# Top-32 attention before a capacity-limited mixture of experts: weights from scores computed a second time, keys on partitions

## The chip, the cores and the metric

The kernel runs on one core of a Trainium2 chip. A core has engines that run side by side, each with its own queue of instructions worked off in order: TensorE (matrix products, written to PSUM), VectorE, ScalarE and GpSimd (element-wise work and reductions), and queues that start transfers between HBM and SBUF. They meet through semaphores. In profiles TensorE is PE (PEld is its weight load), VectorE DVE, ScalarE ACT, GpSimd POOL. The metric is the time of one execution on the device in microseconds; lower is better.

## The reference

Only the first block is touched by the change: attention in which each query keeps its 32 largest scores. Its output, with the heads side by side, feeds a mixture of experts (argmax gate, at most 80 tokens per expert, two products), which stays as it is.

```python
batch, n_heads, seq, head_dim = (8, 8, 576, 64)
...
def _attn_ref(q, k, v):
    top_k = 32
    scale = 1.0 / np.sqrt(D)
    scores = scale * np.matmul(q, k.transpose(0, 1, 3, 2))
    kth = np.partition(scores, -top_k, axis=-1)[..., -top_k:-top_k + 1]
    mask = scores >= kth
    scores = np.where(mask, scores, -1000000000.0)
    scores = scores - np.max(scores, axis=-1, keepdims=True)
    attn = np.exp(scores)
    attn = attn / (np.sum(attn, axis=-1, keepdims=True) + 1e-09)
    return np.matmul(attn, v).astype(np.float32)
```

All inputs and outputs are fp32. A row's 32nd largest score has to be found exactly: it decides which keys count.

## The kernel before

Heads are taken in pairs, 32 pairs in all. A pair's q and k are turned so that head dimension lies on partitions, 64 for each of the two heads. A *unit* is 128 queries of one head against all 576 keys: four per head, and a ninth unit that holds the last 64 queries of both heads. That makes 288 units. The steps of one unit:

```python
def front(self, n, t):          # scores of two heads, queries on partitions
    ps = [self.ps_s.tile([P, 2, 512], F32, name="sp", tag="sp") for _ in range(2)]
    for j in range(2):
        for h in range(2):
            nc.tensor.matmul(ps[h][..., j, :HS], lhsT=qT[d, t * P : t * P + m], rhs=kT[d, j * HS : (j + 1) * HS], ...)
    for h in range(2):          # one copy per head, scaled by 2**-48
        nc.scalar.activation(self.s[u]..., ps[h]..., Act.Copy, scale=TINY)

def parts(self, i):             # the 8 largest of each of 6 stretches of 96 keys
    for j in range(NG):
        nc.vector.max(out=cand[:, j, :], in_=s[:, j * S // NG : (j + 1) * S // NG])
        yield

def search(self, i):
    for r in range(G0 // 8):    # the 24 largest of the 48 candidates
        nc.vector.max(out=dst, in_=cand)
        yield
        if r < G0 // 8 - 1:
            nc.vector.match_replace(out=cand, in_to_replace=dst, in_values=cand, imm_value=LOW)
            yield
    # how many scores reach the 24th candidate, and s with those out of the way
    nc.vector.scalar_tensor_tensor(out=y, in0=s, scalar=w9[:, 7:8], in1=s, op0=Alu.is_ge, op1=Alu.subtract,
                                   accum_out=self.cnt[:, i : i + 1])
    yield
    nc.vector.max(out=w9[:, 8:], in_=self.y.pop(i))      # the next 8
    yield
    nc.vector.scalar_tensor_tensor(out=pick, in0=past, scalar=self.cnt[:, i : i + 1], in1=w9[:, 7:],
                                   accum_out=self.thr[i], op0=Alu.is_equal, op1=Alu.mult)   # the 32nd largest
    yield

def turn_sign(self, i):
    nc.gpsimd.tensor_scalar(y, y, -1.0, 0.0, op0=Alu.mult, op1=Alu.add)

def drop(self, i):              # d = s where it counts, far below the rest
    nc.scalar.activation(low, s, Act.Relu, bias=thr[:, 0:1], scale=-1.0)
    nc.gpsimd.tensor_scalar(low, low, BIG, top[:, 0, 0:1], op0=Alu.mult, op1=Alu.add)
    nc.gpsimd.tensor_tensor(out=self.d[i], in0=s, in1=low, op=Alu.subtract)

def turn_w(self, i):            # keys to partitions, five chunks of 116, then exp
    for c in range(NC):
        nc.tensor.transpose(w[:CK, c * P : (c + 1) * P], dd[:, k0 : k0 + CK], ident)
    nc.scalar.activation(self.wT[i]..., w[:CK, : NC * P], Act.Exp, scale=scale / TINY)

def back(self, i, n, t, h):     # product with v and a column of ones, 64 queries at a time
    for c, (j, hh, r, p) in order:
        nc.tensor.matmul(pw[...], lhsT=wT[:, c, r : r + TL], rhs=self.vb[...][:, c, hh, :], ...)
    nc.scalar.copy(xu[:, t, h, :], pw[:, o : o + D + 1])
```

The program is laid out step by step, one unit entering at each step, so that VectorE's instructions of neighbouring units lie between each other (`G` is a chunk maximum of the newest unit, the small letters are the next instructions of older ones):

```python
for c in "GbGcGdGeGgGfah":
    ...
self.drop(i - 3)
self.turn_sign(i - 1)
self.turn_w(i - 4)
if t == 1 and h == 0: self.turn(n + 1)
if units[i + 2][2] != 1: self.front(*units[i + 2][:2])
self.back(i - 4, *units[i - 4])
...                             # norm: division, output rows, gate logits of finished head pairs
```

In the text, *chunk maximum* is the instruction `G`, *whole-row maximum* the one over `y`, *front* the score products, *group* what `turn_w` puts on TensorE, *product with V* what `back` does.

Of the kernel before, what the change touches and what calls it, by code (L numbers as in the profile page):

```python
# [21 lines left out]
BIG = 2.0 ** 100  # L22
# [3 lines left out]
def kernel(  # L26
# [28 lines left out]
    CK = 116  # L55
    NC = 5
    DUP = NC * CK - S
# [32 lines left out]
    past = count_up("past", TOP_K - G0 + 1, pattern=[[-1, TOP_K - G0 + 1]], base=TOP_K, channel_multiplier=0)  # L90
# [23 lines left out]
    class Attention:  # L114


        def __init__(self, stack, lean):
            self.lean = lean
            pool = lambda name, bufs, **kw: stack.enter_context(tc.tile_pool(name=name, bufs=bufs, **kw))
            self.nat, self.qkp, self.rows = pool("nat", 1), pool("qkp", 2), pool("rows", 2)  # L120
            self.small, vpool = pool("small", 4), pool("vpool", 1)
            self.ps_s, self.ps_w = pool("ps_s", 2, space=PSUM), pool("ps_w", 2, space=PSUM)
            self.qk, self.turned, self.lg = {}, {}, {}
            self.s, self.top, self.y, self.thr, self.d, self.w, self.wT, self.xu = ({} for _ in range(8))
            if not lean:

                self.cnt = vpool.tile([P, NU], F32, name="cnt")

            self.vb = []
            for j in range(1 if lean else 3):  # L130
                t = vpool.tile([CK, NC, 2, D + 1], F32, name=f"vb{j}")
                nc.gpsimd.memset(t[:, :, :, D : D + 1], 1.0)
                nc.gpsimd.memset(t[:DUP, NC - 1, :, :], 0.0)
                self.vb.append(t)

            self.xTb = []
            for j in range(1 if lean else 2):
                t = vpool.tile([P, NK * P], F32, name=f"xT{j}")
                nc.gpsimd.memset(t[:, S:], 0.0)
                self.xTb.append(t)  # L140

        def load(self, n, b, hp):
# [11 lines left out]
            t = self.vb[n % len(self.vb)]  # L154
            e = (NC - 1) * CK
            for h in range(2):
                nc.sync.dma_start(
                    t[:, : NC - 1, h, :D], v[one, 2 * hp + h, :e, :].rearrange("o (c p) d -> p (o c) d", p=CK))
            nc.sync.dma_start(
                t[DUP:CK, NC - 1, :, :D], v[one, 2 * hp : 2 * hp + 2, e:, :].rearrange("o h p d -> p (o h) d"))  # L160
            self.qk[n] = tiles

        def turn(self, n):

            ts_ = []
            for src, name in zip(self.qk.pop(n), ("qT", "kT")):
                src = src.rearrange("p c h d -> p c (h d)")
                t = self.qkp.tile([P, S], F32, name=name, tag=name)
                ps = self.ps_w.tile([P, 1024], F32, name="tp", tag="w")
                for c in range(NF):  # L170
                    nc.tensor.transpose(ps[:, c * P : (c + 1) * P], src[:, c, :], ident)  # L171
                nc.tensor.transpose(ps[:, NF * P : S], src[:TL, NF, :], ident[:TL, :TL])
# [4 lines left out]
        def front(self, n, t):  # L177
# [4 lines left out]
            ps = [self.ps_s.tile([P, 2, 512], F32, name="sp", tag="sp") for _ in range(2)]  # L182
            off = [0, 0] if t < NF else [0, TL]
            for j in range(2):
                for h in range(2):
                    d = slice(D * h, D * h + D)
                    nc.tensor.matmul(ps[h][off[h] : off[h] + m, j, :HS], lhsT=qT[d, t * P : t * P + m],  # L187
                                     rhs=kT[d, j * HS : (j + 1) * HS], start=True, stop=True)
            for h in range(2):
                u = i + h if t < NF else i  # L190
                if t < NF or h == 0:
                    self.s[u] = self.rows.tile([P, S], F32, name="s", tag="s", bufs=3 if self.lean else 7)
                o = slice(off[h], off[h] + m)
                nc.scalar.activation(self.s[u][o, :].rearrange("p (j c) -> p j c", j=2), ps[h][o, :, :HS], Act.Copy,  # L194
                                     scale=TINY)
# [10 lines left out]
        def search(self, i):  # L206
# [4 lines left out]
            for r in range(G0 // 8):  # L211
                dst = top[:, r, :] if r < G0 // 8 - 1 else w9[:, :8]
                nc.vector.max(out=dst, in_=cand)  # L213
                yield
                if r < G0 // 8 - 1:
                    nc.vector.match_replace(out=cand, in_to_replace=dst, in_values=cand, imm_value=LOW)  # L216
                    yield
            y = self.y[i] = self.rows.tile([P, S], F32, name="y", tag="y")
            nc.vector.scalar_tensor_tensor(out=y, in0=s, scalar=w9[:, 7:8], in1=s, op0=Alu.is_ge, op1=Alu.subtract,  # L219
                                           accum_out=self.cnt[:, i : i + 1])  # L220
            yield
            nc.vector.max(out=w9[:, 8:], in_=self.y.pop(i))  # L222
            yield
            pick = self.small.tile([P, TOP_K - G0 + 1], F32, name="pick", tag="pick")
            self.thr[i] = self.small.tile([P, 1], F32, name="thr", tag="thr")
            nc.vector.scalar_tensor_tensor(out=pick, in0=past, scalar=self.cnt[:, i : i + 1], in1=w9[:, 7:], accum_out=self.thr[i],  # L226
                                           op0=Alu.is_equal, op1=Alu.mult)
            yield

        def turn_sign(self, i):  # L230
            y = self.y[i]
            nc.gpsimd.tensor_scalar(y, y, -1.0, 0.0, op0=Alu.mult, op1=Alu.add)  # L232

        def search_all(self, i):
# [9 lines left out]
            self.thr[i] = top[:, TOP_K // 8 - 1, 7:8]  # L244

        def drop(self, i):

            s, top, thr = self.s.pop(i), self.top.pop(i), self.thr.pop(i)
            low = self.rows.tile([P, S], F32, name="low", tag="low")
            nc.scalar.activation(low, s, Act.Relu, bias=thr[:, 0:1], scale=-1.0)  # L250
            nc.gpsimd.tensor_scalar(low, low, BIG, top[:, 0, 0:1], op0=Alu.mult, op1=Alu.add)  # L251
            self.d[i] = self.rows.tile([P, S], F32, name="d", tag="d")
            nc.gpsimd.tensor_tensor(out=self.d[i], in0=s, in1=low, op=Alu.subtract)  # L253

        def turn_w(self, i):

            dd = self.d.pop(i)
            w = self.w[i] = self.ps_w.tile([P, 1024], F32, name="pw", tag="w")
            for c in range(NC):
                k0 = c * CK if c < NC - 1 else S - CK  # L260
                nc.tensor.transpose(w[:CK, c * P : (c + 1) * P], dd[:, k0 : k0 + CK], ident)  # L261
            self.wT[i] = self.rows.tile([CK, NC, P], F32, name="wT", tag="wT")
            nc.scalar.activation(self.wT[i].rearrange("p c r -> p (c r)"), w[:CK, : NC * P], Act.Exp, scale=scale / TINY)  # L263

        def back(self, i, n, t, h):

            wT, pw = self.wT.pop(i), self.w.pop(i)
            if t == 0 and h == 0:
                self.xu[n] = self.rows.tile([P, NK, 2, D + 1], F32, name="xu", tag="xu")
            xu = self.xu[n]  # L270
            o = NC * P
            parts = [(0, h, 0, 0), (0, h, TL, TL)] if h < 2 else [(0, 0, 0, 0), (1, 1, TL, 0)]
            order = [(c, x) for c in range(NC) for x in parts] if h < 2 else [(c, x) for x in parts for c in range(NC)]
            for c, (j, hh, r, p) in order:
                nc.tensor.matmul(pw[p : p + TL, o + j * (D + 1) : o + (j + 1) * (D + 1)], lhsT=wT[:, c, r : r + TL],  # L275
                                 rhs=self.vb[n % len(self.vb)][:, c, hh, :], start=(c == 0), stop=(c == NC - 1))
            if h < 2:
                nc.scalar.copy(xu[:, t, h, :], pw[:, o : o + D + 1])  # L278
            else:
                nc.scalar.copy(xu[:TL, t, :, :].rearrange("p h d -> p (h d)"), pw[:TL, o : o + 2 * (D + 1)])  # L280

        def norm(self, n, b, hp, bi, nb):
# [20 lines left out]
            ps = self.ps_w.tile([P, 1024], F32, name="tp", tag="w")  # L303
            for c in range(NF):
                nc.tensor.transpose(ps[:, c * P : (c + 1) * P], xn[:, c, :], ident)
            nc.tensor.transpose(ps[:, NF * P : S], xn[:TL, NF, :], ident[:TL, :TL])
            xT = self.xTb[n % len(self.xTb)]
            nc.scalar.copy(xT[:, :S], ps[:, :S])
            yield
            ps = self.ps_w.tile([P, 1024], F32, name="tp", tag="w")  # L310
# [48 lines left out]
        def run(self, slow):  # L359
# [7 lines left out]
            later = []  # L367

            def step(i):
                if i < NU:  # L370
# [3 lines left out]
                    if t in (1, 3) and h == 0 and slow and n:  # L374
                        slow.pop(0)()
                    first[i] = self.parts(i)
                for c in "GbGcGdGeGgGfah":
# [8 lines left out]
                    elif i - (2 if c in "gh" else 1) in second:  # L386
                        next(second[i - (2 if c in "gh" else 1)])
                if 0 <= i - 3 < NU:
                    self.drop(i - 3)
                if 0 <= i - 1 < NU:  # L390
                    self.turn_sign(i - 1)
                if 0 <= i - 4 < NU:
                    self.turn_w(i - 4)
                if i < NU:
                    if t == 1 and h == 0 and n + 1 < NP:
                        self.turn(n + 1)
                    if i + 2 < NU and units[i + 2][2] != 1:
                        self.front(*units[i + 2][:2])
                if 0 <= i - 4 < NU:
                    self.back(i - 4, *units[i - 4])  # L400
# [294 lines left out]
```

## Time and profile before

The time is 1470.59 us, the median of three runs (1466.25 to 1477.74). The profiled execution spans 1469.7 us. Busy time of each engine in two stretches of it, with the mean granted TensorE clock:

| stretch, us | PE | DVE | ACT | POOL | PEclk |
|---|---|---|---|---|---|
| 600 to 800 (attention) | 149.42 | 186.82 | 111.76 | 149.64 | 0.79 |
| 1340 to 1470 (experts) | 97.99 | 26.14 | 10.39 | 15.39 | 0.84 |

How the lines of a profile are read: a group's line has source line, engine and operation, what is written from what, shapes, the number of instructions, then busy time in us and mean duration in ns, then the engine's idle time just before them and what ended most of it. In the timeline, the columns are start and length in us, engine, line, operation and count; instructions of one line that follow each other are merged. Durations of instructions in a pipeline overlap, so the distance from start to start may be shorter than the duration. The clock record says which share of its full clock TensorE was granted, in periods of 3.413 us; it takes only the values 0.5 and 1.0 here.

### The profile page before, as it was taken

The page shows a single profiled execution, that of the slowest core. Times are in us where ns is not written, and L with a number is a line of the kernel's source. Part 1 is how long each engine was busy: PE and PEld are TensorE (multiplying, and loading weights), DVE is VectorE, ACT ScalarE, POOL GpSimd, SP SyncE. Part 2 cuts the span into 40 slices and gives each one's busy share as a digit, 9 for nine tenths or more (in the row PEclk, how much of TensorE's full clock was granted, in tenths as well). Part 3 has the DMA queues.
Part 4 walks back from the last instruction along what each step waited for, and adds up shares of the span by engine and source line. Part 5 has one row for each costly group of instructions (what it writes and reads, how often), then busy time and mean ns, then how long its engine had stood idle before and what let it go on. Part 6 is the DMA issues. An engine that isn't in the chain of part 4 may idle for free.

```text
span 1469.7 us, 32849 instructions
## 1 busy us (share of the span) xinstructions
PE 1068.7 (73%) x11502; PEld 799.3 (54%) x11502; DVE 1241.3 (84%) x5385; ACT 721.5 (49%) x1341; POOL 961.4 (65%) x1072
## 2 busy tenths in 40 slices
PE   6677777777777777777777777787777777631887
PEld 4455555555555555555555555555555555531887
DVE  6999999999999998899999989989999889948110
ACT  4555555555555555555555555554555555410010
POOL 4777777777777777777777777777776787710110
PEclk8888877887788787787877778777887778755799
DMA  5023222222122112222222111101111110030470
GB/s 130 2 91 91 91 76 62 62 62 62 33 58 60 53 48 60 62 62 62 62 62 62 48 32 30 30 12 32 34 34 33 33 34 9 10 123 0 130 266 27
DMA packets 153294, 85.59 MB, mean 58 GB/s; under 512 B 117024, under 2 KB 135456, under 8 KB 153120
## 3 DMA queue, kind: packets, MB, share of 16 engines
q1 hardware_dynamic: 152096, 80.78, 19.5%
q0 software_dynamic: 1024, 2.62, 0.6%
q8 instruction: 93, 1.52, 0.4%
q14 instruction: 81, 0.66, 0.2%
HBM read 63.19 MB, written 20.19 MB: 57 GB/s over the span
## 4 chain that ended last, share of the span: by engine, by line
DVE 58%; POOL 15%; PE 14%; issue 10%; ACT 1%; DMA 0%; SPq 0%; POOLq 0%; DVEq 0%; ACTq 0%
DVE y L219 18%; DVE cand L202 12%; DVE w L222 9%; DVE pick L226 8%; POOL d L253 7%; DVE cand L216 4%; POOL low L251 4%; POOL y L232 4%; DVE top L213 3%; PE yp L603 3%; PE sp L187 2%; PE pw L275 2%; PE pw L261 2%; DVE w L213 1%; DVE top L478 1%
## 5 line engine op out<-in xcount | busy, mean ns | idle before, releaser
L253 POOL TENSOR_TENSOR d<-s,low 128x576 f32<-128x576 f32 x288 | 459.5, 1596 | 24.0
L202 DVE MAX8 cand<-s 128x8 f32<-128x96 f32 x1728 | 416.4, 241 | 12.9 <-ACT s L194 12.9
L261 PE MATMUL pw<-ident,d 128*116 128x128 f32 x1440 | 275.8, 335 | 167.9 <-POOL d L253 167.5
L275 PE MATMUL pw<-vb,wT 116*64 116x65 f32 x5760 | 294.6, 252 | 136.1 <-ACT wT L263 136.1
L275 PEld LDWEIGHTS pw<-vb,wT 116*64 116x64 f32 x5760 | 250.4, 161 | 262.7 <-ACT wT L263 202.7
L251 POOL TENSOR_SCALAR low<-low,top 128x576 f32<-128x576 f32 x288 | 223.5, 776 | 208.8 <-ACT low L250 184.7
L219 DVE SCALAR_TENSOR_TENSOR y<-s,w 128x576 f32<-128x576 f32 x288 | 347.7, 1207 | 0.0
L261 PEld LDWEIGHTS pw<-ident,d 128*116 128x116 f32 x1440 | 193.6, 165 | 201.5 <-POOL d L253 190.7
L250 ACT ACTIVATE low<-s,thr 128x576 f32<-128x576 f32 x288 | 223.9, 777 | 129.2 <-DVE pick L226 126.5
L222 DVE MAX8 w<-y 128x8 f32<-128x576 f32 x288 | 213.3, 741 | 86.4 <-POOL y L232 86.4
L187 PE MATMUL sp<-kT,qT 64*128 64x288 f32 (+1 forms) x1280 | 279.3, 563 | 1.5 <-ACT s L194 0.7
L232 POOL TENSOR_SCALAR y<-y 128x576 f32<-128x576 f32 x288 | 196.6, 683 | 98.8 <-DVE y L219 98.8
L194 ACT ACTIVATE s<-sp 128x576 f32<-128x576 f32 (+1 forms) x320 | 193.7, 648 | 129.2 <-PE sp L187 128.2
L263 ACT ACTIVATE wT<-pw 116x640 f32<-116x640 f32 x288 | 201.0, 698 | 56.0 <-PE pw L261 51.3
L226 DVE SCALAR_TENSOR_TENSOR pick<-past,cnt,w 128x9 f32<-128x9 f32 x288 | 183.6, 638 | 0.1
L187 PEld LDWEIGHTS sp<-kT,qT 64*128 64x128 f32 (+1 forms) x1280 | 145.4, 233 | 63.1 <-issue 41.7
L213 DVE MAX8 top<-cand 128x8 f32<-128x48 f32 x576 | 111.5, 194 | 0.1
L278 ACT COPY xu<-pw 128x65 f32<-128x65 f32 x256 | 55.7, 217 | 110.0 <-PE pw L275 107.0
L216 DVE MATCH_REPLACE8 cand<-top,cand 128x48 f32<-128x48 f32 x576 | 107.2, 186 | 0.0
L615 POOL DMA_INDIRECT out_dram<-y,idx_s x8 | 7.4, 930 | 79.0 <-DVE y L614 79.0
L213 DVE MAX8 w<-cand 128x8 f32<-128x48 f32 x288 | 53.8, 187 | 0.0
L171 PE MATMUL tp<-ident,kn 128*128 128x128 f32 x128 | 34.7, 425 | 23.1 <-ACT qT L173 22.6
(160 smaller groups left out, 799.1 us busy)
## 6 DMA issues: line engine op xcount, KB each, us to landing
w<-in_moe_w_dram SPq DMA_DIRECT2D x32, 512.0 KB
w<-in_moe_w_dram SPq DMA_DIRECT2D x8, 2048.0 KB
out_dram<-zero SPq DMA_DIRECT2D x9, 1024.0 KB
qn<-in_q_dram SPq DMA_DIRECT2D x64, 128.0 KB
kn<-in_k_dram SPq DMA_DIRECT2D x64, 128.0 KB
xd<-xn SPq DMA_DIRECT2D x32, 256.0 KB
vb<-in_v_dram SPq DMA_DIRECT2D x64, 116.0 KB
vb<-in_v_dram SPq DMA_DIRECT2D x32, 56.0 KB
```

What stands on the lines that cost most here:

```text
L187: nc.tensor.matmul(ps[h][off[h] : off[h] + m, j, :HS], lhsT=qT[d, t * P : t * P + m], rhs=kT[d, j * HS : (j + 1) * HS], start=True, stop=True)
L202: nc.vector.max(out=cand[:, j, :], in_=s[:, j * S // NG : (j + 1) * S // NG])
L213: nc.vector.max(out=dst, in_=cand)
L219: nc.vector.scalar_tensor_tensor(out=y, in0=s, scalar=w9[:, 7:8], in1=s, op0=Alu.is_ge, op1=Alu.subtract, accum_out=self.cnt[:, i : i + 1])
L222: nc.vector.max(out=w9[:, 8:], in_=self.y.pop(i))
L226: nc.vector.scalar_tensor_tensor(out=pick, in0=past, scalar=self.cnt[:, i : i + 1], in1=w9[:, 7:], accum_out=self.thr[i], op0=Alu.is_equal ...
L232: nc.gpsimd.tensor_scalar(y, y, -1.0, 0.0, op0=Alu.mult, op1=Alu.add)
L250: nc.scalar.activation(low, s, Act.Relu, bias=thr[:, 0:1], scale=-1.0)
L251: nc.gpsimd.tensor_scalar(low, low, BIG, top[:, 0, 0:1], op0=Alu.mult, op1=Alu.add)
L253: nc.gpsimd.tensor_tensor(out=self.d[i], in0=s, in1=low, op=Alu.subtract)
L261: nc.tensor.transpose(w[:CK, c * P : (c + 1) * P], dd[:, k0 : k0 + CK], ident)
L275: nc.tensor.matmul(pw[p : p + TL, o + j * (D + 1) : o + (j + 1) * (D + 1)], lhsT=wT[:, c, r : r + TL], rhs=self.vb[n % len(self.vb)][:, c, ...
```

## The change

Weights are needed with keys on partitions. Before, the masked scores were made with queries on partitions and turned by transposes. After, the scores are computed a second time with keys on partitions, and the mask (0 for a kept key up to the row's maximum, 1 for a dropped one, in bf16) is multiplied into the same PSUM by `minus`, the identity times -2**48, so that exp gives zero for what is dropped. The count of scores above the 24th candidate comes from ScalarE's Sign and its sum, and the same signs, multiplied by `s` on GpSimd, put the larger scores out of the way; GpSimd's other two passes and ScalarE's Relu go. Two heads share a score copy (`ps` is now one tile of four banks) and a group (`ab`, two banks, one buffer; `cc`, one bank, two buffers).

```diff
+    minus = const.tile([P, P], BF16, name="minus")
+    nc.scalar.mul(minus, ident, -1.0 / TINY)
...
-            self.ps_s, self.ps_w = pool("ps_s", 2, space=PSUM), pool("ps_w", 2, space=PSUM)
+            self.ps_s, self.ps_w, self.ps_c = (pool(n, k, space=PSUM) for n, k in (("ps_s", 1), ("ps_w", 1), ("ps_c", 2)))
...
+            nc.scalar.activation(s[:, : g * S].rearrange("p (j c) -> p j c", c=HS), ps[:, : 2 * g, :HS], Act.Copy, scale=TINY)
...
+                if r == G0 // 8 - 1:
+                    y = self.rows.tile([P, S], F32, name="y", tag="y", bufs=3)
+                    cnt = self.small.tile([P, 1], F32, name="cnt", tag="cnt")
+                    nc.scalar.activation(y, s, Act.Sign, bias=w9[:, 7:8], scale=-1.0, accum_out=cnt)
+                    nc.gpsimd.tensor_tensor(out=y, in0=s, in1=y, op=Alu.mult)
...
-            nc.vector.scalar_tensor_tensor(out=y, in0=s, scalar=w9[:, 7:8], in1=s, op0=Alu.is_ge, op1=Alu.subtract,
-                                           accum_out=self.cnt[:, i : i + 1])
...
-        def turn_sign(self, i):
-            y = self.y[i]
-            nc.gpsimd.tensor_scalar(y, y, -1.0, 0.0, op0=Alu.mult, op1=Alu.add)
...
-            nc.scalar.activation(low, s, Act.Relu, bias=thr[:, 0:1], scale=-1.0)
-            nc.gpsimd.tensor_scalar(low, low, BIG, top[:, 0, 0:1], op0=Alu.mult, op1=Alu.add)
-            nc.gpsimd.tensor_tensor(out=self.d[i], in0=s, in1=low, op=Alu.subtract)
+            self.mask[i] = self.rows.tile([P, S], BF16, name="mask", tag="mask", bufs=3)
+            nc.vector.tensor_scalar(self.mask[i], s, self.thr[:, i : i + 1], top[:, 0, 0:1], op0=Alu.is_lt, op1=Alu.add)
...
-                nc.tensor.transpose(w[:CK, c * P : (c + 1) * P], dd[:, k0 : k0 + CK], ident)
+            for c in range(NK):
+                for h in range(2):
+                    nc.tensor.matmul(ab[:, h, c, :m] if c < NF else cc[d, :m], lhsT=masks[h][:, ks], rhs=eye[h],
+                                     start=True, stop=False)
+                for h in range(2):
+                    nc.tensor.matmul(ab[:, h, c, :m] if c < NF else cc[d, :m], lhsT=kT[d, ks], rhs=qT[d, rows],
+                                     start=False, stop=True)
+            nc.scalar.activation(wT[:, : 2 * NF, :m], ab..., Act.Exp, scale=scale)
+            nc.scalar.activation(wT[:, 2 * NF, :m], cc[:, :m], Act.Exp, scale=scale)
...
-                for c in "GbGcGdGeGgGfah":
+                back = dict(a=0, b=1, c=1, d=1, e=1, g=2, h=3, m=3)      # how many steps a letter lies behind
+                for c in "GbGcGdGehGmGga":                                # h: pick, m: mask, g: whole-row maximum
...
+                j = i - 3
+                if 0 <= j < NU and units[j][2]:
+                    self.turn_w(*units[j][:2])
+                self.fronts = i + 2 < NU and units[i + 2][2] != 1
+                if self.fronts:
+                    self.front(*units[i + 2][:2])
+                elif due:
+                    self.turn(due.pop())
+                j = i - 4
+                if 0 <= j < NU and units[j][2]:
+                    self.back(*units[j][:2])
```

Products with V take 128 keys per chunk and a last chunk of 64 in place of five of 116.

## The prediction

> **What bounds the kernel now.** I read the page first: engines, granted clock, costliest groups.
>
> ```profile
> PE 1068.7 (73%) x11502; PEld 799.3 (54%) x11502; DVE 1241.3 (84%) x5385; ACT 721.5 (49%) x1341; POOL 961.4 (65%) x1072
> ...
> PEclk8888877887788787787877778777887778755799
> ...
> L253 POOL TENSOR_TENSOR d<-s,low 128x576 f32<-128x576 f32 x288 | 459.5, 1596 | 24.0
> ...
> L261 PE MATMUL pw<-ident,d 128*116 128x128 f32 x1440 | 275.8, 335 | 167.9 <-POOL d L253 167.5
> ...
> L251 POOL TENSOR_SCALAR low<-low,top 128x576 f32<-128x576 f32 x288 | 223.5, 776 | 208.8 <-ACT low L250 184.7
> L219 DVE SCALAR_TENSOR_TENSOR y<-s,w 128x576 f32<-128x576 f32 x288 | 347.7, 1207 | 0.0
> ...
> L222 DVE MAX8 w<-y 128x8 f32<-128x576 f32 x288 | 213.3, 741 | 86.4 <-POOL y L232 86.4
> ...
> L226 DVE SCALAR_TENSOR_TENSOR pick<-past,cnt,w 128x9 f32<-128x9 f32 x288 | 183.6, 638 | 0.1
> ```
>
> VectorE has nearly no idle time in attention, which lasts from about 12 to 1284 us: 288 units, 4.42 us each, 39.8 us per head pair of nine. But `pick`, on nine numbers, cannot need 638 ns. The views of these two lines give minimum, median and maximum:
>
> ```profile
> L226 DVE SCALAR_TENSOR_TENSOR pick<-past,cnt,w x288: 201/209/1244, 17.7 to 1283.9; 128x9 f32<-128x9 f32 x144
> ```
>
> ```profile
> L219 DVE SCALAR_TENSOR_TENSOR y<-s,w x288: 790/1209/1971, 13.8 to 1279.4; 128x576 f32<-128x576 f32 x144
> ```
>
> Mean minus minimum is 0.44 us for `pick` and 0.42 us for `y`: 246 us in 288 units during which VectorE stands inside an instruction while GpSimd works. So the bound is VectorE, slowed by GpSimd. From starts in the timeline, one unit without blocking is six chunk maxima at 0.165, two replacements at 0.17, three maxima over 48 at 0.11, `y` 0.80 with its accumulator read, the whole-row maximum 0.67 and `pick` 0.25: 3.38 us.
>
> Then the timeline of TensorE, and busy time by stretches of one clock period each:
>
> ```profile
> 716.05 0.80 PE L275 MATMUL pw<-vb,wT 116*64 116x65 f32 x20 [0.85 <-ACT wT L263]
> ...
> 718.01 0.76 PE L261 MATMUL pw<-ident,d 128*116 128x128 f32 x5 [0.37 <-POOL d L253]
> 718.70 1.24 PE L187 MATMUL sp<-kT,qT 64*128 64x288 f32 x8
> 719.87 0.80 PE L275 MATMUL pw<-vb,wT 116*64 116x65 f32 x20
> 720.61 1.28 PE L313 MATMUL tp<-wg,xT 128*128 128x8 f32 x10
> ```
>
> ```profile
> 701.40:704.80 3.40, 0.92 (x22) 0.66 (x20) 3.40 (x19) 1.48 (x4) 3.07 (x8) 1.00 0.00 0
> 704.80:708.20 3.40, 2.39 (x11) 1.55 (x13) 2.77 (x14) 1.07 (x2) 3.22 (x4) 0.50 0.00 0
> 708.20:711.60 3.40, 3.40 (x31) 2.18 (x27) 3.40 (x17) 2.17 (x4) 3.12 (x4) 0.50 0.00 0
> 711.60:715.00 3.40, 2.63 (x34) 1.87 (x33) 2.71 (x16) 2.67 (x5) 3.31 (x3) 0.99 0.69 172
> ```
>
> (The first pair after the colon is length and PE busy; the third number from the end is the granted clock.) A stretch with PE busy 0.92 of 3.40 us is followed by half clock, a full one by full clock. Laying each matmul's streaming time (columns times two for fp32, over the clock) on every 3.41 us period of the clock record, the rule is sharp: periods before a fall had 0.16 to 0.36, full-clock periods that stayed 0.41 or more; a rise came after 0.76 or more.
>
> **The Trainium skill.** "SBUF — State Buffer", Who interferes with whom: a VectorE instruction with two SBUF inputs, or in a two-port mode, contends with GpSimd's reads for a shared port, and the loser waits out the whole instruction. The 201 and 1244 ns of `pick` agree. "TensorEngine Tiling (Array Packing)", Key Properties: changing the tiling mode drains TensorE. Agrees: after the last 128x116 transpose at full clock the next row-tiled scores start 95 ns later than its streaming ends (median of 73 places), and 92 to 98 ns is found at all other mode changes; at half clock 130 to 138. "TensorE: Matmul & The Clock Gate", Part 1: a 3413 ns activity window switches between 4/8 and 8/8. Agrees, with the thresholds above being this trace's. "VectorE: DVE Perf Modes", The perf-mode tier table: an fp32 `tensor_scalar` in SBUF runs at 2×, and The TRN2 errata gives 58 + 576/2 cycles at 0.96 GHz; no such instruction of this size is in the trace, so 0.36 us is an estimate.
>
> **The change by parts.**
>
> VectorE loses `y` (0.80) and gets the mask (0.36): 2.94 us a unit, 26.5 us per head pair. Its second two-source instruction is gone; `pick` and mask stay exposed to GpSimd.
>
> GpSimd loses 683 + 776 ns per unit and keeps one product like L253 (1.40 unblocked): 880 us of work become about 405.
>
> ScalarE loses `low` (777) and gets Sign, which I take as equal; scores are copied for two heads at once, exps are merged. From 648 ns for 576 and 698 for 640 elements, 1152 take about 1.13 us and the exp of 1024 + 128 about 1.3. Per head pair about 23 us; no bound.
>
> TensorE loses five transposes per unit and gets, per pair of units and per each of five key chunks: two mask products (weights 54, streams 53 + 54 ns at full clock), a mode change (95), row-tiled fp32 scores (exposed weight load 107, streams 2 x 107 for both heads side by side), a change back (95). That is 0.67 us per chunk, 0.54 for the last narrow one: 3.2 us per group at full clock, 5.9 at half. Only 320 of 670 ns stream, a share of 0.48. Per head pair, at full clock: four groups and a narrow one (2.8) 15.6, score fronts 5 x 1.16 = 5.8, products with V 5.6, turning q, k and x 2.2, logits 1.2: 30.4 us. At half clock 57. The transposes removed were about 9 x 0.75 = 6.8 us at full clock. So TensorE work rises by 9 us per head pair and passes VectorE's 26.5.
>
> It also comes on the critical path. In the step order the new group waits for the mask made in the same step, and stands in TensorE's queue ahead of the score front for two steps later. Loop at full clock, from a mask: group 3.2, semaphore and pipeline end 0.2, both exps 1.3 on ScalarE (the front runs meanwhile), the score copy 1.13, then VectorE's 2.0 from the first chunk maximum to the next mask: 8.0 us for two units. VectorE alone needs 5.9. Sign waits in ScalarE's queue behind exp and copy, so the GpSimd product falls on `pick` and mask: about 0.8 more. Following the nine steps of a head pair this way, with the single score and `ab` buffers, gives about 39 us at full clock throughout, against 39.8 now. The VectorE saving is eaten by the loop.
>
> Full clock will not hold. After a product with V, TensorE waits some 2 us for the next mask, then runs a group that streams 0.48 of the time: a window with 2.2 us idle and 1.2 us of group has a share of 0.17, far below 0.36. A fall per head pair is certain there; another is likely at the narrow group, which waits for the one `ab` buffer. A group at half clock streams 0.52, so it cannot bring the clock back; only front plus product (4.7 us at half clock, share about 0.87) can, and it fills a window about two times in three. I count per head pair +4.7 us for group, front and product after the first fall, +2 in the middle, +5.9 around the last two groups: 39 + 12 = 51 us.
>
> Sum: 12 us of start, 32 x 51 = 1632, and a tail of about 185 as now (the expert stage is untouched): 1830 us. I shade this down to 1690, because twelve of the 51 us rest on where free-running windows fall, and because a pipeline may hide waits that I added in a row.
>
> **Rivals.**
>
> A: VectorE stays the bound and simply gets cheaper. For it: the 246 us of blocking, the 86 us waiting for `y`, and 0.44 us less work. It would need TensorE to hold full clock: 32 x (26.5 to 30) + 197 = 1045 to 1160 us. Against: TensorE alone needs 30.4 us at a clock that it has never held for more than four windows in attention.
>
> B: TensorE, now busier, keeps full clock, and the loop sets the time: 32 x (34 to 39) + 197 = 1290 to 1450 us. For it: more real streaming than now, 0.6 if TensorE never waits. Against: every wait ahead of a group costs the clock.
>
> C: half clock nearly throughout: 32 x 57 + 197 = 2020 us. Against: front, product and turning in a row stream over 7 us at half clock once per head pair and lift it.
>
> **Range and chances.** My own chain gives 1830; B's lower half is what a saving needs (under 1441 us is under 38.9 us per head pair). I give B and A together 0.15 below that line, 0.07 for about the same, 0.78 for slower. The range, 1420 to 1880, goes from B's upper end to a little above my chain.
>
> **What would show it.** Right: TensorE's idle time before the mask product released by VectorE's mask, VectorE's idle before the chunk maximum released by the score copy (12.9 us now, over 150 then), mean clock at or below 0.8, PE busy over 1200 us, mask product and second scores at about 0.67 us a chunk at full clock, GpSimd under 40% of the span, `pick` under 400 ns in the mean. Wrong: a mean clock over 0.9, or a group of ten mask and ten score products in under 2.5 us at full clock because mode changes cost less here than the 95 ns; then B holds. A time below 1300 would say that the loop does not close as I read it from the order of instructions.

## The result, and the profile after

The changed kernel takes 1613.26 us in the median (1612.21 to 1616.73), the kernel before 1469.85 (1466.25 to 1477.74) on the same chip: a ratio of 1.097, with a 95% interval of 1.092 to 1.102. The change costs 143 us. Of the six parts of the page, four carry the story. Engines, granted clock, the chain that ended last (by engine), and the costliest groups, in that order:

```profile
PE 1311.5 (81%) x14862; PEld 936.5 (58%) x14862; DVE 1124.7 (70%) x5095; ACT 682.4 (42%) x1374; POOL 513.0 (32%) x501
...
PEclk9888788887888887888878888878888788775699
...
PE 70%; DVE 17%; ACT 11%; issue 2%; POOL 0%; DMA 0%; POOLq 0%; DVEq 0%; ACTq 0%
...
L219 POOL TENSOR_TENSOR y<-s,y 128x576 f32<-128x576 f32 x288 | 416.7, 1447 | 891.9 <-ACT y L218 888.1
L202 DVE MAX8 cand<-s 128x8 f32<-128x96 f32 x1728 | 428.7, 248 | 253.2 <-ACT s L195 253.1
...
L265 PE MATMUL ab<-minus,mask 128*128 128x128 bf16 (+1 forms) x1280 | 197.8, 233 | 150.7 <-DVE mask L249 132.2
...
L249 DVE TENSOR_SCALAR mask<-s,thr,top 128x576 bf16<-128x576 f32 x288 | 264.9, 920 | 0.3
```

VectorE fell from 84% to 70% busy and GpSimd from 65% to 32%, and it did not help: VectorE now stands idle for 253.1 us waiting for score copies (12.9 before). TensorE rose from 1068.7 to 1311.5 us busy. The last chain runs 70% through TensorE; in the kernel before it ran 58% through VectorE and 14% through TensorE. The clock record looks much as before: 0.83 in the mean over the span, 0.78 before. The chain and the chunk maximum of the kernel before:

```profile
DVE 58%; POOL 15%; PE 14%; issue 10%; ACT 1%; DMA 0%; SPq 0%; POOLq 0%; DVEq 0%; ACTq 0%
...
L202 DVE MAX8 cand<-s 128x8 f32<-128x96 f32 x1728 | 416.4, 241 | 12.9 <-ACT s L194 12.9
```

The two lines that showed VectorE blocked by GpSimd, `pick` and now the mask, each in its own view (minimum, median, maximum in ns; first and last start in us):

```profile
L249 DVE TENSOR_SCALAR mask<-s,thr,top x288: 559/579/1816, 20.0 to 1426.7; 128x576 bf16<-128x576 f32 x144
```

```profile
L227 DVE SCALAR_TENSOR_TENSOR pick<-past,cnt,w x288: 203/214/1108, 19.7 to 1426.4; 128x9 f32<-128x9 f32 x144
```

Two readings follow. The 32 head pairs of attention take (1426.7 - 20.0) / 32 = 44.0 us each (39.8 before). And blocking survives: the mask's mean is 920 ns over a minimum of 559, `pick`'s 487 over 203, together 288 x (0.361 + 0.284) = 186 us against 246 before.

TensorE's timeline of the changed kernel, around a wait for the mask:

```profile
737.81 0.23 PE L265 MATMUL ab<-minus,mask 128*128 128x128 bf16 x1
741.90 0.23 PE L265 MATMUL ab<-minus,mask 128*128 128x128 bf16 x1 [3.85 <-DVE mask L249]
742.06 0.49 PE L269 MATMUL ab<-qT,kT 64*128 64x128 f32 x4
...
742.70 0.80 PE L269 MATMUL ab<-qT,kT 64*128 64x128 f32 x4
```

The group needs the masks of two units. It runs the first mask product, stands 3.85 us at the second, and 0.8 us after it goes on, its second scores take 0.80 us in place of 0.49: the clock has fallen. Such a wait comes about once per head pair: 34 waits of 3.85 us make up nearly all of the 132.2 us that TensorE waits there. Where the clock is whole, a chunk takes 0.64 us from scores to scores:

```profile
708.70 0.49 PE L269 MATMUL ab<-qT,kT 64*128 64x128 f32 x4
709.12 0.29 PE L265 MATMUL ab<-minus,mask 128*128 128x128 bf16 x2
709.34 0.49 PE L269 MATMUL ab<-qT,kT 64*128 64x128 f32 x4
```

### The profile page after: what moved, and what is told of

The parts are those of the page before. It is cut to its first block, busy times and chain, and to the rows that moved or that the text cites. A ratio compares the mean times of both kernels' runs of the same rounds, so it can differ in the third digit from the quotient of the medians.

```text
span 1610.5 us, 38356 instructions
## 1 busy us (share of the span) xinstructions
PE 1311.5 (81%) x14862; PEld 936.5 (58%) x14862; DVE 1124.7 (70%) x5095; ACT 682.4 (42%) x1374; POOL 513.0 (32%) x501
## 4 chain that ended last, share of the span: by engine, by line
PE 70%; DVE 17%; ACT 11%; issue 2%; POOL 0%; DMA 0%; POOLq 0%; DVEq 0%; ACTq 0%
PE ab L269 19%; PE sp L190 15%; PE ab L265 9%; PE cc L287 9%; ACT s L195 5%; DVE mask L249 4%; DVE cand L202 4%; PE cc L269 4%; DVE pick L227 3%; PE sp L165 3%; PE lp L322 2%; PE yp L613 2%; ACT wT L272 2%; DVE cand L222 2%; PE cc L265 2%
## 5 line engine op out<-in xcount | busy, mean ns | idle before, releaser
L219 POOL TENSOR_TENSOR y<-s,y 128x576 f32<-128x576 f32 x288 | 416.7, 1447 | 891.9 <-ACT y L218 888.1
L202 DVE MAX8 cand<-s 128x8 f32<-128x96 f32 x1728 | 428.7, 248 | 253.2 <-ACT s L195 253.1
L269 PE MATMUL ab<-qT,kT 64*128 64x128 f32 (+1 forms) x2560 | 359.2, 363 | 0.0
L272 ACT ACTIVATE wT<-ab 128x1024 f32<-128x1024 f32 (+1 forms) x160 | 150.2, 939 | 415.8 <-PE ab L269 413.7
L265 PE MATMUL ab<-minus,mask 128*128 128x128 bf16 (+1 forms) x1280 | 197.8, 233 | 150.7 <-DVE mask L249 132.2
L190 PE MATMUL sp<-kT,qT 64*128 64x288 f32 (+1 forms) x1280 | 275.3, 565 | 48.3 <-ACT s L195 25.7
L269 PEld LDWEIGHTS ab<-qT,kT 64*128 64x128 f32 x2560 | 228.1, 218 | 68.5 <-issue 18.5
L249 DVE TENSOR_SCALAR mask<-s,thr,top 128x576 bf16<-128x576 f32 x288 | 264.9, 920 | 0.3
L265 PEld LDWEIGHTS <-mask 128*128 128x128 bf16 (+1 forms) x1600 | 103.8, 104 | 255.7 <-DVE mask L249 145.7
L287 PEld LDWEIGHTS cc<-vb,wT 128*64 128x64 f32 x4608 | 210.5, 163 | 67.2 <-issue 52.7
L195 ACT ACTIVATE s<-sp 128x1152 f32<-128x1152 f32 (+1 forms) x160 | 165.7, 1035 | 181.0 <-PE sp L190 180.8
L287 PE MATMUL cc<-vb,wT 128*64 128x65 f32 x4608 | 241.6, 251 | 0.0
L218 ACT ACTIVATE y<-s,w 128x576 f32<-128x576 f32 x288 | 222.8, 774 | 18.7 <-DVE w L213 18.6
L190 PEld LDWEIGHTS sp<-kT,qT 64*128 64x128 f32 (+1 forms) x1280 | 140.6, 233 | 128.9 <-ACT s L195 55.8
```

What stands on the lines that cost most here:

```text
L190: nc.tensor.matmul(o, lhsT=qT[d, t * P : t * P + m], rhs=kT[d, j * HS : (j + 1) * HS], start=True, stop=True)
L195: nc.scalar.activation(s[:, : g * S].rearrange("p (j c) -> p j c", c=HS), ps[:, : 2 * g, :HS], Act.Copy, scale=TINY)
L218: nc.scalar.activation(y, s, Act.Sign, bias=w9[:, 7:8], scale=-1.0, accum_out=cnt)
L219: nc.gpsimd.tensor_tensor(out=y, in0=s, in1=y, op=Alu.mult)
L249: nc.vector.tensor_scalar(self.mask[i], s, self.thr[:, i : i + 1], top[:, 0, 0:1], op0=Alu.is_lt, op1=Alu.add)
L265: nc.tensor.matmul(ab[:, h, c, :m] if c < NF else cc[d, :m], lhsT=masks[h][:, ks], rhs=eye[h], start=True, stop=False)
```

## The experiments

The theory: time is set by a loop through the step order. A group waits for the mask and stands in TensorE's queue ahead of the next front; the front's copy lets VectorE go on to the next mask. The loop is lengthened by the clock, which falls in the waits, by the mode changes inside the group, and by GpSimd blocking. Rivals: TensorE simply has too much work; the Sign half, not the second scores, is what costs; the clock just follows and costs nothing. One more is not put to a run: that the single score buffer holds the front back. The profile gives it little room, as TensorE's front waits only 25.7 us for the copy that frees the buffer (55.8 by its weight loads). All ratios are to the kernel before, with 95% intervals.

### The front ahead of the group

```diff
-                self.turn_w(...)                     # group
-                if fronts: self.front(...)
-                elif due: self.turn(due.pop())
+                if fronts: self.front(...)
+                self.turn_w(...)
+                if not fronts and due: self.turn(due.pop())
```

> The changed kernel with one difference: in each step the score front of two steps ahead is put into TensorE's queue before the group of mask products and second scores, not behind it. Loop theory (VectorE waits for scores that stand behind a group which waits for VectorE's mask): VectorE's wait for the score copy falls from 253 us to under 80, the front fills TensorE's idle time ahead of the mask, and the time falls to 1420 to 1510 us. Throughput theory (TensorE's busy time of 1312 us is the bound, whatever the order): the same work in another order, 1580 to 1625 us. Blocking theory (GpSimd's product holding pick and mask up sets the pace): no change, 1590 to 1625 us, mask still 0.9 us in the mean.

1381.38 us, ratio 0.941 [0.938, 0.944]: better than the expected range, and 232 us less than the changed kernel with the same TensorE instructions. The clock is 0.90. Page lines for engines and chain, and the group of the chunk maximum:

```profile
PE 1188.6 (86%) x14862; PEld 858.8 (62%) x14862; DVE 1050.2 (76%) x5095; ACT 673.7 (49%) x1374; POOL 505.6 (37%) x501
...
DVE 45%; PE 39%; POOL 7%; ACT 6%; issue 3%; DMA 0%; POOLq 0%; DVEq 0%; ACTq 0%
...
L202 DVE MAX8 cand<-s 128x8 f32<-128x96 f32 x1728 | 428.1, 248 | 16.8 <-ACT s L195 16.8
```

The wait for score copies is gone, 253.1 to 16.8 us. The rival that TensorE has too much work falls: 14862 products before and after the swap. They are 123 us shorter in sum (1311.5 to 1188.6) as more of them ran at full clock: from 200 to 1100 us the clock is 0.92, and 0.83 in the changed kernel. So the 232 us hold two things that this run does not part, the waits that the order spares and the clock that comes back with it; an estimate follows under the clock.

### No mode change in the group

```diff
-                    matmul(ab.., lhsT=masks[h][:, ks], rhs=eye[h], start=True, stop=False)
+                for x in range(2):
+                    for h in range(2):
+                        matmul(ab.., lhsT=masks[h][d, ks], rhs=eye[h][d, :], start=x == 0, stop=False)
```

The mask products here take only 64 of the 128 mask rows, so that they have the row tiles of the scores; every product is issued twice. Half of the masking is left out.

> The changed kernel with the mask products cut to 64 rows each, so that they run in the same row tiles as the second scores; the number of products and of streamed columns stays, but each head's mask is applied from only half of the queries (twice), so half of the masking is left out. The ten changes between 128-row and 64-row products per group go. If a change costs 95 ns at full clock and exposes the next weight load, a group falls from 3.05 us to 1.8 to 2.2 us at full clock, streams about 0.75 of the time, and the mean clock rises above 0.88. Loop theory: 1330 to 1450 us. Throughput theory: the bound falls by 160 groups times 1 us over the clock, 1400 to 1450 us. Blocking theory: 1580 to 1620 us. If mode changes cost little here: 1580 us or more.

1382.36 us, ratio 0.942 [0.939, 0.945], clock 0.90: in the range of the loop theory. From its TensorE timeline:

```profile
703.09 0.49 PE L270 MATMUL ab<-qT,kT 64*128 64x128 f32 x4
703.37 0.32 PE L266 MATMUL ab<-minus,mask 64*128 64x128 bf16 x4
703.48 0.49 PE L270 MATMUL ab<-qT,kT 64*128 64x128 f32 x4
```

A chunk takes 0.39 us in place of 0.64, with more products in it: the two mode changes, with the weight loads that they expose, cost 0.25 us per chunk. Order is unchanged here, so a shorter group alone, with the clock that it brings back, is worth as much as the swap.

### Products sorted by kind

```diff
+            for h in range(2):      # opens a whole bank with zeros
+                matmul(ab[:, h] as 512 columns, lhsT=masks[h][:, :P], rhs=zeros, start=True, stop=False)
+            all mask products; then the narrow chunk's scores, then all other scores
-            per chunk: two mask products, then the scores of both heads
```

Nothing is left out; there are four mode changes per group in place of ten (the narrow chunk has tiles of its own).

> The changed kernel with the products of a group sorted by kind: per head one product of 512 zero columns that opens the bank, then all mask products, then all second scores; four mode changes per group in place of ten, 2 x 213 ns of streaming added at full clock. Nothing is left out. From the durations a group takes about 2.5 us at full clock (3.05 before) and streams 0.74 of it. Loop theory with the clock: 1460 to 1550 us, mean clock above 0.86. Throughput theory: 160 x 0.5 us over the clock less, 1500 to 1530 us. Blocking theory: 1590 to 1620 us.

1426.20 us, ratio 0.971 [0.967, 0.975], clock 0.92: again better than expected. First and last products of a group at full clock, in the changed kernel and then in this one:

```profile
732.23 0.28 PE L265 MATMUL ab<-minus,mask 128*128 128x128 bf16 x2
...
734.96 0.44 PE L269 MATMUL cc<-qT,kT 64*64 64x128 f32 x4
```

```profile
702.96 0.38 PE L263 MATMUL ab<-zero,mask 128*128 128x512 bf16 x1
...
704.26 1.16 PE L271 MATMUL ab<-qT,kT 64*128 64x128 f32 x16
```

A group took 2.46 us (702.96 to 705.42) against 3.17 (732.23 to 735.40). The gain, 187 us in 160 groups, is 1.17 us per group; the group itself is 0.71 shorter at full clock. The rest, by subtraction, would be the clock (0.95 from 200 to 1100 us) and waits that the shorter group no longer causes; no run parts these.

### Both

The swap and the sorting in one kernel.

> Front ahead of the group and products sorted by kind, nothing left out. Loop theory: both shorten what VectorE waits for and what makes the clock fall; 1320 to 1430 us, under the kernel before, VectorE's wait for the score copy under 60 us, mean clock above 0.9. Throughput theory: as the sorted products alone, 1500 to 1530 us. Blocking theory: 1590 to 1620 us.

1276.13 us (1272.31 to 1277.87), ratio 0.868 [0.865, 0.872], again less than expected. It leaves nothing out, and is the best complete version here, 194 us under the kernel before. Engines, clock and chain, from its page:

```profile
PE 1013.3 (80%) x15054; PEld 792.2 (62%) x15182; DVE 1100.8 (86%) x5095; ACT 666.2 (52%) x1374; POOL 508.5 (40%) x501
...
PEclk9999999999999999999999999999999999855999
...
DVE 69%; PE 18%; POOL 4%; issue 4%; ACT 3%; DMA 0%; POOLq 0%; ACTq 0%; SPq 0%; DVEq 0%
```

The clock is whole throughout attention, and VectorE is the bound again (863 of 900 us busy from 200 to 1100 us). Attention takes (1093.3 - 20.4) / 32 = 33.5 us per head pair.

### Which half of the change pays: the count by Sign

Three kernels ask this. First, the changed kernel with the old count (VectorE's `is_ge`/`subtract`, GpSimd's sign pass):

```diff
-   nc.scalar.activation(y, s, Act.Sign, bias=w9[:, 7:8], scale=-1.0, accum_out=cnt)
-   nc.gpsimd.tensor_tensor(out=y, in0=s, in1=y, op=Alu.mult)
+   nc.vector.scalar_tensor_tensor(out=y, in0=s, scalar=w9[:, 7:8], in1=s, op0=Alu.is_ge, op1=Alu.subtract, accum_out=cnt)
+   nc.gpsimd.tensor_scalar(y, y, -1.0, 0.0, op0=Alu.mult, op1=Alu.add)
```

The constants that `pick` compares the count with change along.

> The changed kernel with the count of before put back: VectorE's two-source instruction makes y and the count, GpSimd only turns the sign; the weights stay as changed. Loop theory: VectorE's part of the loop grows by 0.8 us per unit, and ScalarE loses Sign and its accumulator read (0.97 us) from the queue that the score copy stands in; where the loop is bound by TensorE's group, most of the 0.8 us is hidden: 1600 to 1680 us. Throughput theory: TensorE bound, no change, 1600 to 1625 us. Blocking theory: the GpSimd pass falls from 1.4 to 0.68 us, but a second two-source instruction joins; 1600 to 1700 us.

1614.29 us, ratio 1.100 [1.095, 1.104]: the same as the changed kernel. VectorE works 136 us more (1124.7 to 1261.0) and the time does not move, so the sum of VectorE's work was not what the time hung on. It does not show that VectorE's part of the loop costs nothing: the run also takes Sign out of ScalarE's queue and most of the blocking off `pick` (231 ns in the mean, 487 before), and such gains can make up for the added instruction. The run with the small product, below, shows that time on this part does count.

Second, the kernel before with the new count alone: the same lines the other way round, ScalarE's `low` and GpSimd's two passes kept.

> The kernel before with the other half of the change alone: count by Sign with its sum, GpSimd multiplies y by s, weights still through Relu, two GpSimd passes and transposes. VectorE loses 0.80 us per unit plus the blocking of that instruction (0.42), GpSimd gets 1.40 for 0.68 and then needs 1.40 + 0.78 + 1.40 = 3.58 us per unit unblocked, about 3.9 with blocking. Loop and throughput theory alike (this kernel has no group on TensorE): GpSimd becomes the bound at 3.6 to 4.0 us per unit, 1250 to 1370 us. Blocking theory: pick waits longer, as GpSimd is busy nearly all the time, 1400 to 1480 us.

1572.57 us, ratio 1.070 [1.066, 1.074]: 202 us above the range of the loop and throughput theories, and 93 above that of the blocking theory. VectorE is only 61% busy. The chain of this kernel, from its page, and the first line of its waits:

```profile
POOL 55%; issue 19%; PE 17%; ACT 4%; DVE 3%; DMA 0%; POOLq 0%; SPq 0%; ACTq 0%; DVEq 0%
```

```profile
DVE w L221 <- POOL y L231: 449.0, 186, 4.5
```

I had added up loads. GpSimd is 70% busy, which leaves room, but it is a queue, and a loop closes through it:

```profile
702.19 0.75 POOL L250 TENSOR_SCALAR low<-low,top 128x576 f32<-128x576 f32 x1
703.02 1.40 POOL L252 TENSOR_TENSOR d<-s,low 128x576 f32<-128x576 f32 x1
704.37 1.40 POOL L231 TENSOR_TENSOR y<-s,y 128x576 f32<-128x576 f32 x1
710.25 0.74 POOL L250 TENSOR_SCALAR low<-low,top 128x576 f32<-128x576 f32 x1 [4.48 <-ACT low L249]
```

`y` of one unit queues behind `low` and `d` of an older one, `low` waits for the pick of that unit, and the pick for its own `y`. GpSimd stands idle 4.48 us here, and 253.6 us in all for `low`, in a kernel whose chain runs 55% through it. No run changes the order of this queue, so that the loop is the cause is read from the profile and not tested; 19% of the chain has no cause that the profile shows.

Third, the old count in the swapped and sorted kernel, where VectorE is the bound.

> The front ahead of the group and the sorted products, but the count and the displaced scores made as before the change: VectorE's two-source instruction and GpSimd's sign pass instead of Sign and the product. Where TensorE's loop set the time this swap made no difference. Where VectorE sets it (69% of the chain of the reordered and sorted kernel, at 1276 us), theory A, the Sign half pays there, says: 288 x 0.8 us come back on VectorE, less some 0.1 to 0.2 us per unit of blocking that the one-input GpSimd pass does not cause: 1400 to 1470 us. Theory B, what Sign frees on VectorE is taken back by waiting on the GpSimd product and its blocking (0.22 us per mask, 0.37 per pick): 1270 to 1330 us.

1399.40 us, ratio 0.952 [0.948, 0.956], 0.6 us below theory A's range: here the Sign half is worth 123 us (1399.4 to 1276.1). One piece of code costs 103 us, nothing, or gains 123, by what else bounds the kernel.

### What GpSimd's blocking costs

The changed kernel, its GpSimd product on 8 of 576 columns; the larger scores are then mostly not put out of the way, so the selection is left out in effect, while all other work stays.

```diff
-   nc.gpsimd.tensor_tensor(out=y, in0=s, in1=y, op=Alu.mult)
+   nc.gpsimd.tensor_tensor(out=y[:, :8], in0=s[:, :8], in1=y[:, :8], op=Alu.mult)
```

> The changed kernel with GpSimd's product cut to 8 of 576 columns; the larger scores are then not put out of the way and the threshold is wrong, so the selection is left out in effect, while all other instructions stay. No blocking is left: mask 0.58 us and pick 0.21 us in the mean, the whole-row maximum waits for nothing. Loop theory: the part of the loop between first chunk maximum and mask shortens by what blocking added on it (0.5 to 0.8 us per pair of units), with fewer falls of the clock 1480 to 1570 us. Throughput theory: 1590 to 1615 us. Blocking theory: the blocked 180 us go in full and more, under 1430 us.

1498.85 us, ratio 1.017 [1.011, 1.023]. Mask and `pick` come down to 584 and 214 ns in the mean, and the time by 114 us. So 169 us less inside VectorE's instructions (1124.7 to 956.2 us busy) give back 114: VectorE's part of the loop counts. Still it is no faster than the kernel before: the loop remains, with 334.2 us of waiting for score copies. The same edit in the swapped and sorted kernel:

> Front ahead of the group and products sorted by kind, as in the 1276 us kernel, and GpSimd's product cut to 8 of 576 columns (selection left out in effect). With the loop open, VectorE is the bound, so what blocking costs is paid in full: mask falls from 0.80 to 0.58 us and pick from 0.58 to 0.21, 170 us less of VectorE's time, less what TensorE and ScalarE then hold up: 1110 to 1180 us. If blocking is hidden behind other waits: 1240 to 1280 us.

1221.80 us, ratio 0.832 [0.829, 0.834]: 54 us less than with the whole product, and not the 96 to 166 I had expected. I had counted the blocked time as if nothing stood behind it. The chain is then TensorE 43%, VectorE 37%, ScalarE 14%, and VectorE waits 103.7 us (36.4 with the whole product) for the product. That takes only 240 ns here, and GpSimd waited for Sign in all 288 units: it is Sign that is late.

Why does the mask stand still at all, with one source and a bf16 output? The swapped and sorted kernel, its mask written with an accumulator output (which leaves out the subtraction of the row's maximum):

```diff
-   nc.vector.tensor_scalar(mask, s, thr, top, op0=Alu.is_lt, op1=Alu.add)
+   nc.vector.tensor_scalar(mask, s, thr, top, op0=Alu.is_lt, op1=Alu.add, accum_out=junk)
```

> The reordered and sorted kernel with one thing more on the mask: it also writes its row sums, and by that the row's maximum goes unsubtracted (weights before division differ by a factor per row). If the mask stands still behind the GpSimd product because it runs in a doubled mode that an accumulator output takes away, its mean (801 ns, minimum 560) comes down to near its minimum, whatever that then is (0.6 to 0.85 us), and maximum and mean stay close; 1230 to 1290 us. If it stands still for another reason, its maximum remains near 1.75 us and its mean 0.2 us over its minimum: 1280 to 1340 us.

1291.85 us, ratio 0.879 [0.876, 0.883]. First the mask's view in the swapped and sorted kernel, then with the accumulator output:

```profile
L249 DVE TENSOR_SCALAR mask<-s,thr,top x288: 560/579/1748, 20.4 to 1093.3; 128x576 bf16<-128x576 f32 x144
```

```profile
L250 DVE TENSOR_SCALAR_CACHE_REDUCE mask<-s,thr,top x288: 856/872/875, 20.0 to 1112.2; 128x576 bf16<-128x576 f32 x144
```

From 560 to 1748 ns it becomes 856 to 875: no longer blocked, but slower than the blocked mean of 801. (The time alone, 2 us above the first range and inside the second, would not have decided it.) This is what the Trainium skill, "SBUF — State Buffer", Who interferes with whom, says: `tensor_scalar` can enter a two-port mode and contend with GpSimd, but not in the form that also writes its accumulator. The trace agrees. For the kernel the blocked form is better by 16 us; the other also brings an accumulator read of 83 ns per mask.

### What the clock costs

Zeros multiplied on TensorE ahead of each group, into banks that the group then overwrites. They bring nothing but activity and do not wait for the mask.

```diff
+            for x in range(6):      # or 12
+                matmul(ab[:, x % 2] as 512 columns, lhsT=minus, rhs=zeros, start=True, stop=True)
             for c in range(NK):     # the group, as in the changed kernel
```

> The changed kernel with six products of zeros (128 x 512, bf16, 0.21 us each at full clock, 1.28 us together) ahead of each group, which overwrites what they write. They wait for the banks of the group, not for the mask, so most run while TensorE would stand idle. They bring nothing but activity: 160 x 1.28 = 205 us of work more. Theory that the granted clock costs part of the 143 us: the clock rises above 0.87 and the time falls in spite of the added work, to 1450 to 1570 us. Theory that only the order of waits counts and the clock follows it without costing much: time is the same or longer, 1610 to 1750 us.

> The same with twelve products of zeros, 2.56 us at full clock, which is more than the usual 1.7 us of waiting for the mask. Clock theory: clock above 0.93, but about 0.9 us per group now lies on the loop: 1500 to 1640 us, above the run with six unless that one left the clock low. Theory of the order alone: 1700 to 1950 us.

1654.22 us, ratio 1.125 [1.120, 1.130], at a clock of 0.91; and 1750.91 us, ratio 1.193 [1.188, 1.197], at 0.97. The clock rose as expected and the time did not fall: both of my numbers for the clock theory missed, and those of the theory of the order alone hold. I had thought that most of the zeros would fit into TensorE's waits for a mask, spread over the groups; but these lie nearly all in one place per head pair (34 waits of 3.85 us). But "costs nothing" does not hold either: 205 us of added products lengthened the run by 41, and 409 by 138. Mean busy time in 200 to 1100 us, of the changed kernel and then of the kernel with twelve products (after the length: PE, PEld, DVE, ACT, POOL, clock, DMA share, GB/s):

```profile
200.00:1100.00 900.00, 758.55 (x8007) 528.19 (x8004) 677.31 (x3168) 424.14 (x854) 314.93 (x290) 0.83 0.18 48
```

```profile
200.00:1100.00 900.00, 813.70 (x8303) 521.87 (x8393) 597.19 (x2861) 383.37 (x775) 280.51 (x261) 0.99 0.16 45
```

Per head pair, with twelve: (1560.4 - 20.0) / 32 = 48.1 us, of which 60 x 0.213 = 12.8 are zeros. TensorE is idle 0.157 x 44.0 = 6.9 us per head pair without them and 0.096 x 48.1 = 4.6 with them, so 2.3 us of zeros went into idle time and 10.5 lay in the way. Without them, a loop at full clock is 48.1 - 10.5 = 37.6 us. That is an estimate, and it says that half clock costs the changed kernel some 6.4 of its 44.0 us per head pair, 200 us in all.

The same reckoning parts the swap's gain, again as an estimate. The run with twelve leaves 43.5 - 12.8 = 30.7 us of busy TensorE per head pair for all but the zeros, nearly all at full clock. The swapped kernel takes (1193.6 - 20.0) / 32 = 36.7 us per head pair, and TensorE is busy for 0.904 of it, 33.2 us. Half clock would then cost 2.5 us there in place of 6.4. Of the 7.3 us that the swap gains per head pair, some 3.9 would be the clock's, and 3.4 the waits that the order spares. No run here held the changed kernel's clock up without adding work.

## Why the prediction was right, and what was mis-sized

The prediction was 1690 us, in a range of 1420 to 1880, with slower at 0.78. The changed kernel took 1613 us. The direction and the mechanism hold: the loop through TensorE's queue, and a clock that falls in its waits. The term for the clock errs in size, by about a factor of two.

- **The number.** The prediction's own chain gave 1830 us, 217 too many; the clock term makes up 32 x (12 - 6.4) = 179 of it, by the estimate above. The 1690 came from taking 140 us off, for windows that fall freely and waits that a pipeline may hide, with no count behind it. That it lies within 5% is owed to this and is in part luck.
- **The bound before.** The bound was VectorE slowed by GpSimd. Most of the expected relief did not come: blocking went from 246 to 186 us, as the product still falls on `pick` and the mask. I had put this at 0.8 us per two units; taking the product away gives 114 us / (32 x 4.5) = 0.8, though this holds what the clock gained too. But "`pick` under 400 ns" was wrong: it is 487.
- **VectorE's saving.** I had the mask at 0.36 us, an estimate from a formula of the Trainium skill, "VectorE: DVE Perf Modes", The TRN2 errata, where it also says that this formula puts the time of a single instruction too low. The trace agrees: it takes 0.58 unblocked (0.50 from start to start). A unit is 0.14 to 0.22 us dearer than my 2.94. The mask lies on the loop, so this counts here too; how much, no run shows.
- **The group on TensorE.** 0.67 us a chunk was predicted, 0.64 measured; 3.2 us a group, 3.17 measured. That mode changes make up much of it is shown by the run without them (0.39). All of TensorE's work at full clock was put at 30.4 us per head pair; the run with twelve gives 30.7. At half clock a group was put at 5.9 us; there a chunk takes 1.06 (second scores start at 699.11 and 700.17) and the narrow one 0.73, about 5.0 us in sum.
- **The loop.** Predicted 39 us per head pair at full clock, about 37.6 by the estimate above. (The terms written down for two units add up to 7.8 us, not to 8.0.) That the load alone is not the cause is shown by the swap, which keeps every product and gains 232 us.
- **The clock: the term that was mis-sized.** I added 12 us per head pair; the estimate is 6.4. My extras (4.7 + 2 + 5.9) need about 25 us at half clock per head pair. A mean clock of 0.83 means half clock for 0.34 of the time, 15.0 us per head pair, which can add 7.5 at most. The clock record shows what I had wrong: three places per head pair where the clock falls. From 20 to 1426 us it falls 64 times, twice per head pair. And TensorE does not wait some 2 us for each mask, but 3.85 us about once per head pair. The rule itself nearly held: by the prediction's reckoning of streaming time, the clock here fell after periods with a share of up to 0.38, stayed full after 0.39 or more, and rose after 0.72 or more (0.36, 0.41 and 0.76 before). The mean clock, predicted at 0.8 or less, was 0.83. The first mask at 20.0, 32 x 43.96, and 183.8 us from the last mask to the end make the 1610.5 us of the profiled run.
- **The rivals.** A falls: VectorE got cheaper and waited. B, the loop at full clock, would have been 32 x 37.6 + 197 = 1400 us: the loop was right, the clock did not hold. C falls by the clock record. That order and sorting would each bring the clock back as well was not in the prediction, and each gained more than I expected of it.

The other marks came out as predicted: TensorE's wait for the mask (132.2 us, 145.7 by its weight loads), VectorE's for the score copy (253.1), PE busy over 1200 us, GpSimd at 32%.

## What to carry to other kernels

When work is moved off the busiest engine, the loop that the move creates has to be added up in the order of the queues: here putting the front ahead of the group turned a loss of 10% into a gain of 6% without changing one instruction (about half of it, by the estimate, through the clock), and with the products sorted it became 13%. Before removing an operation from a path, ask what the removed time stands in front of; the Sign count was worth -103, 0 or +123 us in three surroundings. An engine that is 70% busy can still carry most of the last chain, as GpSimd did with 55%; that its queue made a new unit's work wait behind an old unit's is read from the profile, not tested.

## What the runs showed of the hardware

- A pair of mode changes between 128x128 and row-tiled products costs 0.25 us per chunk at full clock (0.64 to 0.39), weight loads that they expose included; I had 0.19 as the changes proper.
- Zeros count as activity for the clock: with twelve products of zeros per group, it is at 0.99 from 200 to 1100 us, and at 0.83 without them.
- A 128x576 `tensor_scalar` from fp32 to bf16 with two per-row scalars takes 0.58 us on VectorE, 0.87 with an accumulator output; only the first was stopped by GpSimd's product (maximum 1.75 and 0.875).
- GpSimd's pass of one source stops it too, but for less: with the old count in the swapped and sorted kernel, the mask has a minimum of 578, a median of 881 and a maximum of 901 ns. `pick` is not stopped there (226 and 232).
